# Eleven expert passes whose second layer is seven half-size products

## The chip, the cores and the metric

The program runs on one core of one Trainium2 chip, as one launch. The time is the device time of that core in microseconds (us); the median of three runs of the kernel before is 2035.59 us (2035.21 to 2037.2). Engines: TensorE (PE, with its weight loads PEld), VectorE (DVE), ScalarE (ACT), GpSimd (POOL) and SyncE (SP), which issues the DMA transfers. Inputs and outputs are in HBM, tiles in SBUF, matmul results in PSUM.

## The reference

```python
# q, k, v: (4, 8, 576, 64); heads 0-3 see a band of 32 keys, heads 4-7 every 4th of 128
scores = scale * q @ k.T;  attn = softmax(where(mask, scores, -1e9));  a = attn @ v
x = a.transpose(0, 2, 1, 3).reshape(2304, 512)

P = exp(x @ w_gate - max)                 # (2304, 8), 8 experts
for _ in range(8):                        # Sinkhorn
    P /= P.sum(1, keepdims=True) + 1e-9
    P /= P.sum(0, keepdims=True) + 1e-9
    P *= N / E
out = sum over e of P[:, e:e+1] * (maximum(x @ w1[e], 0) @ w2[e])   # w1 512x1024, w2 1024x512

h = out @ w_in                            # 512x2048
g = where(h >= 1, h, where(h <= -1, 0, (h + 1)**2 / 4))
y = g @ w_out                             # 2048x512, result (2304, 512) float32
```

The last two weight matrices arrive as 64-bit floats and are converted in the kernel.

## The kernel before

The hidden width is cut into units of 512 (`UF`): 16 expert units (two per expert) and 4 units of the final feed-forward layer (FFN). Tokens go in three passes of 768 (`PASS`), halves of 384 (`HALF`) and tiles of 128. Every fp32 operand is split into a high and a low fp32r part; `product` (L267) multiplies them with three matmuls: high x high, high x low, low x high.

Unit 0 is computed for all tokens beside the attention (`first_unit`), in plain form. Every other unit is a run (u, k) of unit u on token pass k: expert units 1 to 15 for k = 0, 1, 2, then the four FFN units for k = 0, 1, 2, 57 runs in all. In a run, `first_layer` makes x times w1 as seven half-size products (a Strassen-Winograd scheme, `ORDER` = 1, 5, 6, 2, 7, 3, 4); the operands of x (`xo`, built once per pass by `build_x`: subtractions on POOL, high parts on ACT, low parts on DVE) and of w1 (`w1o`) are sums and differences of quarters. Results collect in PSUM banks "h" (pa), "t" (pb), "s" and "x" (pc); ACT and DVE join them, and the activation writes the high and low parts of the hidden values into `hs`. `second_layer` then multiplies them by w2 (`w2o`) in plain form: 6 token tiles x 4 chunks x 3 matmuls of 512 columns into six banks; as each tile is complete, DVE scales it by the routing weight and adds it to `acc` (L407), which holds all 18 token tiles in SBUF.

In pass 0 the units are "fresh": w1 and w2 are loaded raw, `prep_w1` (sums on POOL L131, high parts on ACT L104, low parts on DVE L105) and `prep_w2` (L98, L99; quarter by quarter, through a two-quarter stage) make the parts, and these are stored in HBM (`w1_kept`, `w2_kept`) and only reloaded in passes 1 and 2: one 0.5 MB transfer per w1 operand, one of 2 MB for w2. `double_steps` converts the FFN weights in small steps beside runs of pass 1 and 2; `sinkhorn_steps` does the routing iterations beside the runs of units 1 and 2. `turn_steps` (L913) transposes `acc` to be the FFN's input, between the matmuls of a second layer.

The order on each engine is the order of the program text: `tc.manual_schedule()` keeps it, engines take their own instructions in order, and semaphores hold them where data or a buffer are not ready. What runs beside a layer is pulled step by step from generators (`pull`, `drain`) in the loop over `runs`, after each of the 14 turns of a first layer and each of the 24 of a second layer.

## Time and profile before

| | |
|---|---|
| time, median of 3 runs | 2035.59 us |
| the profiled execution | 2036.03 us, span 2034.0 us |
| PE busy | 2003.0 us, 10766 matmuls |
| DVE, ACT, POOL busy | 1182.2, 775.0, 225.9 us |
| granted clock, mean over the span | 0.996 |
| DMA | 425 MB, 209 GB/s |

The span is the time from the first to the last instruction of the profiled execution; the rest of its time lies around it. A busy PE includes the drain of each matmul, which overlaps the next one; the distance from start to start tells its rate. Rows of a DVE or ACT instruction overlap a little in the same way.

### The profile page before, as it was taken

Reading aid. Unit: us, or ns where it says so; the run is one execution under the profiler, and the core shown is the slowest. Engines: PE = TensorE matmul, PEld = TensorE weight load, DVE = VectorE, ACT = ScalarE, POOL = GpSimd, SP = SyncE. Lnnn points to the kernel's source line nnn. Section 1 sums busy time; section 2 is a strip of 40 time slices with the busy share of each in tenths; the row PEclk is TensorE's granted clock in tenths of the full one; section 3 lists DMA queues with packets and bytes.
Section 4 is the critical chain, followed back from the end, with each engine's and each line's share of the span. In section 5 each row is a group of like instructions: output and inputs, shape, how many; then the busy total and the mean of one; then the engine's idle time right before and its main releaser. Section 6 shows DMA issues by size and latency. Waiting matters only on the chain.

```text
span 2034.0 us, 29029 instructions
## 1 busy us (share of the span) xinstructions
PE 2003.0 (98%) x10766; PEld 1803.7 (89%) x10766; DVE 1182.2 (58%) x2334; ACT 775.0 (38%) x1809; POOL 225.9 (11%) x259
## 2 busy tenths in 40 slices
PE   8999989999999999999999999999999999999999
PEld 6888879899998898998998989989989989898898
DVE  6644585766666655664665674633433355655756
ACT  6655434444444423322323323312212334444443
POOL 4212212212212201000002000000000100101000
PEclk9999999999999999999999999999999999999999
DMA  7431256766767665865766867745545446364552
GB/s 170 112 71 50 104 223 243 288 228 258 279 229 261 257 233 212 301 248 227 293 240 233 297 220 270 264 164 203 206 144 220 171 171 227 121 252 156 216 214 87
DMA packets 167501, 425.28 MB, mean 209 GB/s; under 512 B 78529, under 2 KB 78529, under 8 KB 160065
## 3 DMA queue, kind: packets, MB, share of 16 engines
q1 hardware_dynamic: 167360, 423.43, 57.6%
q8 instruction: 85, 1.39, 0.3%
q14 instruction: 56, 0.45, 0.1%
HBM read 309.08 MB, written 114.29 MB: 208 GB/s over the span
## 4 chain that ended last, share of the span: by engine, by line
PE 92%; DVE 4%; ACT 1%; issue 1%; DMA 1%; POOL 0%; DVEq 0%; ACTq 0%; POOLq 0%
PE py L267 46%; PE pa L267 22%; PE pc L267 11%; PE pb L267 6%; PE ph L267 3%; PE s L547 2%; PE px L589 1%; PE pt L515 1%; PE pe L573 1%; DVE r L896 0%; PE pg L680 0%; DVE kept L897 0%; DVE kept L285 0%; DVE hl L901 0%; ACT hh L898 0%
## 5 line engine op out<-in xcount | busy, mean ns | idle before, releaser
L267 PE MATMUL py<-w2o,hh 128*128 128x512 f32 x2736 | 846.2, 390 | 0.0
L267 PEld LDWEIGHTS py<-w2o,hh 128*128 128x128 f32 x2736 | 511.6, 188 | 100.5
L267 PE MATMUL py<-w2o,hl 128*128 128x512 f32 x1368 | 533.0, 390 | 0.0
L267 PE MATMUL pa<-xo,w1o 128*128 128x384 f32 x2736 | 514.9, 335 | 4.6 <-ACT kept L282 3.3
L267 PEld LDWEIGHTS pa<-xo,w1o 128*128 128x128 f32 x2736 | 479.9, 188 | 10.7 <-ACT kept L282 3.7
L282 ACT ACTIVATE kept<-pa 128x384 f32<-128x384 f32 x228 | 112.0, 492 | 556.9 <-PE pa L267 556.2
L407 DVE SCALAR_TENSOR_TENSOR acc<-py,prob,acc 128x512 f32<-128x512 f32 x252 | 178.8, 749 | 236.8 <-PE py L267 232.4
L267 PEld LDWEIGHTS py<-w2o,hl 128*128 128x128 f32 x1368 | 257.1, 188 | 53.6
L267 PE MATMUL pc<-xo,w1o 128*128 128x384 f32 x1368 | 256.7, 335 | 0.7 <-DVE w1o L105 0.7
L267 PEld LDWEIGHTS pc<-xo,w1o 128*128 128x128 f32 x1368 | 239.8, 188 | 1.0 <-DVE w1o L105 1.0
L131 POOL TENSOR_TENSOR raw<-raw 128x256 f32<-128x256 f32 x152 | 130.2, 885 | 873.4 <-DVE raw L213 369.9
L285 DVE TENSOR_TENSOR kept<-pb,kept 128x384 f32<-128x384 f32 x114 | 63.4, 556 | 252.0 <-PE pb L267 251.0
L390 ACT ACTIVATE hh<-kept 128x384 fp32r<-128x384 f32 x270 | 142.1, 526 | 175.3 <-DVE kept L285 174.7
L391 DVE SCALAR_TENSOR_TENSOR hl<-kept,hh 128x384 fp32r<-128x384 f32 x270 | 149.2, 553 | 3.6
L267 PE MATMUL pb<-xo,w1o 128*128 128x384 f32 x684 | 127.7, 334 | 0.0
L267 PEld LDWEIGHTS pb<-xo,w1o 128*128 128x128 f32 x684 | 119.4, 188 | 0.0
L105 DVE TENSOR_TENSOR w1o<-raw,w1o 128x256 fp32r<-128x256 f32 x210 | 97.1, 506 | 27.1 <-ACT w1o L104 27.1
L237 POOL TENSOR_TENSOR xf<-xf 128x768 f32<-128x768 f32 x20 | 37.0, 1870 | 615.1 <-ACT xf L915 612.6
L104 ACT ACTIVATE w1o<-raw 128x256 fp32r<-128x256 f32 x210 | 76.3, 415 | 58.1 <-POOL raw L131 58.1
L99 DVE TENSOR_TENSOR w2o<-raw,w2o 128x512 fp32r<-128x512 f32 x60 | 42.7, 712 | 79.7 <-ACT w2o L98 79.7
L282 ACT ACTIVATE kept<-pc 128x384 f32<-128x384 f32 x114 | 56.2, 493 | 51.1 <-PE pc L267 50.4
L267 PE MATMUL ph<-xo,w1o 128*128 128x384 f32 x288 | 66.9, 358 | 0.0
(139 smaller groups left out, 1670.9 us busy)
## 6 DMA issues: line engine op xcount, KB each, us to landing
w1o<-w_kept SPq DMA_DIRECT2D x294, 512.0 KB, 6.2
w2o<-w_kept SPq DMA_DIRECT2D x42, 2048.0 KB, 7.9
w_kept<-w1o SPq DMA_DIRECT2D x105, 512.0 KB, 4.2
w_kept<-w2o SPq DMA_DIRECT2D x15, 2048.0 KB, 7.3
raw<-in_moe_w_dram SPq DMA_DIRECT2D x15, 1024.0 KB, 6.3
raw<-in_moe_w_dram SPq DMA_DIRECT2D x60, 256.0 KB, 5.5
w_kept<-raw SPq DMA_DIRECT2D x28, 512.0 KB, 2.9
xf<-in_moe_w_in_dram SPq DMA_DIRECT2D x16, 512.0 KB, 5.2
```

What stands on the lines that cost most here:

```text
L99: eng.tensor_tensor(out=lo, in0=raw, in1=hi.bitcast(F32), op=ALU.subtract)
L104: nc.scalar.activation(out=hi, in_=raw, func=AF.Copy)
L105: return lambda: nc.vector.tensor_tensor(out=lo, in0=raw, in1=hi.bitcast(F32), op=ALU.subtract)
L131: nc.gpsimd.tensor_tensor(out=out[:, q], in0=in0[:, q], in1=in1[:, q], op=op)
L237: eng.tensor_tensor(out=o, in0=x, in1=y, op=ALU.subtract)
L267: nc.tensor.matmul(o, lhsT=a(h), rhs=b(l), start=first and n == 0, stop=last and n == 2, skip_group_check=on)
L282: nc.scalar.activation(out=dst, in_=src, func=AF.Copy)
L285: nc.vector.tensor_tensor(out=dst, in0=src, in1=dst, op=ALU.add)
L390: return [lambda: nc.scalar.activation(out=hi, in_=src, func=AF.Relu), lambda: nc.vector.scalar_tensor_tensor(out=lo, in0=src, scalar=0.0, ...
L391: lambda: nc.vector.scalar_tensor_tensor(out=lo, in0=src, scalar=0.0, in1=hi.bitcast(F32), op0=ALU.max, op1=ALU.subtract)]
L407: nc.vector.scalar_tensor_tensor(out=acc[:, t, :], in0=py, scalar=prob[:, t, e:e + 1], in1=acc[:, t, :], op0=ALU.mult, op1=ALU.add)
L547: nc.tensor.matmul(s[:, i, :], lhsT=qd[:, pr, j, :], rhs=kt[:, pr, key0(j):key0(j) + KW], start=not early, stop=not early or i == JG - 1)
```

## The change

Eleven of the expert passes (experts 4 to 7 in pass 1, experts 1 to 7 in pass 2; `WHOLE` names the experts that stay plain in pass 1) are now runs ("e", e, k) of both units of an expert. The two first layers follow each other and leave the hidden values whole in `hid` (ACT only). Then `seven_second` multiplies the 1024-wide hidden matrix by w2 as seven half-size products: 4 chunks x 3 token blocks x 3 matmuls of 256 columns each, into half banks, and DVE adds each block, scaled, to `acc`. The operands of the hidden values are made by `Seven` on DVE (subtractions in place, low parts) and ACT (high parts) at turns written out in `FIRST_WORK` and `SECOND_WORK` (s: subtraction, h: high part, l: low part; operand, piece). Operands rotate through three buffers (`h_buf`, `w2_buf`). The w2 operands come from HBM: quarters from `w2_kept`, now stored in two halves, and four sums from `w2_sums`, which `sum_steps` makes in pass 0 on POOL, ACT and DVE.

To make room, `acc` holds one pass only. First results of unit 0 for passes 1 and 2 go to HBM (`y_kept`) and come back; x of passes 1 and 2 (`x_kept`) and the turned result of each pass (`z_kept`) too. Raw w2 is loaded whole, into `xf`. The operands of a new x are made in place by DVE (`build_in_place`) instead of POOL. The transposes (`turn_steps`) go from the last second layer of a pass into the first layer of the next run, and from bank "h" to "y". The routing iterations get one more turn between the column sum and its matmul, and are pulled in more turns of unit 1. `double_steps` has two stage buffers, fewer pauses, a hold at the end of pass 1, and other turns. Cut to its core:

```diff
-    acc = keep.tile([P, NTILE, DM], F32, name="acc")
+    acc = keep.tile([P, TPP, DM], F32, name="acc")
...
-    w2_kept = [dram.tile([P, 2 * KC * DM], F32, name=f"w2_kept{u}") for u in range(NU)]
+    HD = DM // 2
+    w2_kept = [dram.tile([2, P, 2 * KC * HD], F32, name=f"w2_kept{u}") for u in range(NU)]
+    w2_sums = {e: dram.tile([4, P, 2 * KC * HD], F32, name=f"w2_sums{e}") for e in range(1, E)}
+    x_kept = {k: dram.tile([P, KC * PASS], F32, name=f"x_kept{k}") for k in range(1, NPASS)}
+    y_kept = {k: dram.tile([P, TPP, DM], F32, name=f"y_kept{k}") for k in range(1, NPASS)}
+    z_kept = [dram.tile([P, KC * PASS], F32, name=f"z_kept{k}") for k in range(NPASS)]
...
-    def prep_w2(u, stage):
...
+    def raw_w2(u):
+
+        n = KC * DM
+        at_ = u % 4 * n if u > 1 else KC * PASS
+        return xf.rearrange("p k c x -> p (k c x)")[:, at_:at_ + n]
+
+    def load_raw_w2(u):
+        nc.sync.dma_start(out=raw_w2(u).rearrange("p (c f) -> p c f", c=KC), in_=unit_sources(u)[1])
+
+    def prep_w2(u):
+        for c in TURNS:
+            split(raw_w2(u)[:, c * DM:(c + 1) * DM], (w2o[:, 0, c, :], w2o[:, 1, c, :]), nc.vector)
+            yield
+        for d, (there, here) in enumerate(w2_halves(u)):
+            if d == 0 or u % 2 or u // 2 in WHOLE:
+                nc.sync.dma_start(out=there, in_=here)
 
     TURNS = (0, 2, 1, 3)
 
     def load_w1(u, i):
...
+    SUMS = (7, 6, 5, 3)
+
+    def load_op(e, i, into):
+
+        src = {1: (2 * e, 0), 2: (2 * e + 1, 0), 4: (2 * e + 1, 1)}.get(i)
+        there = w2_sums[e][SUMS.index(i)] if src is None else w2_kept[src[0]][src[1]]
+        nc.sync.dma_start(out=into, in_=there)
+
+    def sum_steps(e, stages):
+
+        n = KC * DM
+        at_ = 2 * e % 4 * n
+        raw = (xf.rearrange("p k c x -> p (k c x)")[:, at_:at_ + 2 * n]
+               .rearrange("p (k c d f) -> p k c d f", k=2, c=KC, d=2))
+        stages = [t[:, :2 * KC * HD].rearrange("p (h c f) -> p h c f", h=2, c=KC) for t in stages]
+        a11, a12, a21, a22 = (raw[:, k, :, d] for d in range(2) for k in range(2))
+        for n_, (out_, in0, in1, op) in enumerate(((a21, a11, a21, ALU.subtract), (a22, a22, a21, ALU.subtract),
+                                                   (a11, a22, a11, ALU.add), (a12, a12, a22, ALU.subtract))):
+            o = stages[n_ % 2]
+            for c in (slice(0, 2), slice(2, 4)):
+                nc.gpsimd.tensor_tensor(out=out_[:, c], in0=in0[:, c], in1=in1[:, c], op=op)
+                yield
+            yield
+            for c in (slice(0, 2), slice(2, 4)):
+                low = high(out_[:, c], (o[:, 0, c], o[:, 1, c]))
+                yield
+                low()
+            nc.sync.dma_start(out=w2_sums[e][n_], in_=words(o).rearrange("p h c f -> p (h c f)"))
...
+    class Seven:
+
+
+
+        def __init__(self, quarters_, into, pieces):
+            b11, b12, b21, b22 = quarters_
+            self.sums = {5: (b11, b12, b11), 6: (b11, b22, b11), 7: (b12, b22, b12), 4: (b21, b21, b11)}
+            self.of = {1: b11, 5: b11, 6: b11, 2: b21, 7: b12, 3: b22, 4: b21}
+            self.into, self.lows = into, {}
+            n = b11.shape[1] // pieces
+            self.cut = [slice(x * n, (x + 1) * n) for x in range(pieces)]
+
+        def sum(self, i, x):
+            dst, in0, in1 = (t[:, self.cut[x]] for t in self.sums[i])
+            nc.vector.tensor_tensor(out=dst, in0=in0, in1=in1, op=ALU.subtract)
+
+        def hi(self, i, x):
+            c, o = self.cut[x], self.into(i)
+            self.lows[i, x] = high(self.of[i][:, c], (o[:, 0, c], o[:, 1, c]))
+
+        def low(self, i, x):
+            self.lows.pop((i, x))()
+
+    def build_in_place():
+        v = xf[:, 0].rearrange("p (k c) (j x) -> p k j c x", k=2, j=2)
+        x = Seven([v[:, kk, j] for kk in range(2) for j in range(2)], lambda i: xo[i], 1)
+        for i in ORDER:
+            for step in (x.sum, x.hi, x.low):
+                if step != x.sum or i in x.sums:
+                    step(i, 0)
+                    yield
...
+    WHOLE = (1, 2, 3)
+
+    FIRST_WORK = {1: "h10 h11", 2: "l10", 3: "l11", 4: "s50", 5: "s51 h50", 6: "h51", 7: "l50", 8: "l51",
+                  12: "s60 s61", 13: "s70 s71"}
+    SECOND_WORK = {(0, 0): "h60 h61", (0, 1): "l60", (0, 2): "l61 h20 h21", (1, 0): "l20", (1, 1): "l21",
+                   (1, 2): "h70 h71", (2, 0): "l70", (2, 1): "l71", (2, 2): "h30 h31", (3, 0): "l30 s40",
+                   (3, 1): "l31 s41", (3, 2): "h40 h41", (4, 0): "l40", (4, 1): "l41"}
+
+    def work(ops, what):
+        for x in what.split():
+            {"h": ops.hi, "l": ops.low, "s": ops.sum}[x[0]](int(x[1]), int(x[2]))
+
+    def seven_second(e, k, buf):
+
+
+        def halves(tags):
+
+            a, b = (bank(t, m, f"q{t}") for t, m in tags)
+            return [a[:, :HD], b[:, :HD], a[:, HD:]]
+
+        chain = {}
+        for n, i in enumerate(ORDER):
+            if i in (1, 5, 2):
+                chain[i] = halves({1: (("y", 2), ("y", 2)), 5: (("t", 2), ("t", 2)), 2: (("s", 1), ("x", 1))}[i])
+            of = {1: 1, 6: 1, 7: 1, 4: 1, 5: 5, 3: 5, 2: 2}[i]
+            d, j = {1: (0, 0), 5: (1, 1), 6: (0, 1), 2: (0, 0), 7: (1, 1), 3: (0, 1), 4: (1, 0)}[i]
+            a, w = buf(n)
+            for t in range(TPH):
+                o = chain[of][t]
+                ts_ = slice(t * P, (t + 1) * P)
+                for c in range(KC):
+                    product(o, lambda h: a[:, h, c, ts_], lambda h: w[:, h, c, :],
+                            of == i and c == 0 and t < 2, c == KC - 1, of != i or t == 2)
+                x = j * TPH + t
+                at_ = acc[:, x, d * HD:(d + 1) * HD]
+                nc.vector.scalar_tensor_tensor(out=at_, in0=o, scalar=prob[:, k * TPP + x, e:e + 1], in1=at_,
+                                               op0=ALU.mult, op1=ALU.add)
+                yield n, t
...
+    def finish_first(py, t):
+        k, x = divmod(t, TPP)
+        here = acc[:, x, :] if k == 0 else at.stage()
+        nc.scalar.activation(out=here, in_=py, func=AF.Copy)
+        if k:
+            nc.sync.dma_start(out=y_kept[k][:, x, :], in_=here)
...
             nc.vector.tensor_reduce(out=cols, in_=prob.rearrange("p t e -> p e t"), axis=AX.X, op=ALU.add)
             yield
             yield
+            yield
...
+        third = late.tile([P, 2 * KC * HALF], F32R, name="third")
+        w2x = late.tile([P, 2 * KC * HD], F32R, name="w2x")
+        h_buf = [x.rearrange("p (h c x) -> p h c x", h=2, c=KC) for x in
+                 (hs[0].rearrange("p c x -> p (c x)"), hs[1].rearrange("p c x -> p (c x)"), third)]
+        w2_all = w2o.rearrange("p h c f -> p (h c f)")
+        w2_buf = [w2_all[:, :2 * KC * HD], w2_all[:, 2 * KC * HD:], w2x]
...
+        hid = wide.rearrange("p (k j c x) -> p k j c x", k=2, j=2, c=KC)
+
+        def act_kept(half_):
+            def act(src, f, j):
+                return [lambda: nc.scalar.activation(out=hid[:, half_, j, f], in_=src, func=AF.Relu)]
+            return act
...
+        def turn_steps(k, more):
+
+
+            z = xf[:, 1]
             for c in range(KC):
                 for j in range(2):
-                    pt = bank("h", 2, f"p2{c}_{j}")[:, :HALF]
+                    pt = bank("y", 2, f"p2{c}_{j}")[:, :HALF]
                     for t in range(TPH):
-                        nc.tensor.transpose(pt[:, t * P:(t + 1) * P],
-                                            acc[:, k * TPP + j * TPH + t, c * P:(c + 1) * P], ident)
-                    nc.scalar.activation(out=xf[:, k, c, j * HALF:(j + 1) * HALF], in_=pt, func=AF.Copy)
+                        nc.tensor.transpose(pt[:, t * P:(t + 1) * P], acc[:, j * TPH + t, c * P:(c + 1) * P], ident)
+                    nc.scalar.activation(out=z[:, c, j * HALF:(j + 1) * HALF], in_=pt, func=AF.Copy)
                     yield
+            nc.sync.dma_start(out=z_kept[k], in_=z.rearrange("p c x -> p (c x)"))
+            if more:
+                nc.sync.dma_start(out=acc, in_=y_kept[k + 1])
...
+        FFN = range(N_MOE, NU)
+        runs = [("u", u, 0) for u in range(1, N_MOE)]
+        for k in range(1, NPASS):
+            runs += [("u", 1, k)]
+            for e in range(1, E):
+                runs += [("u", 2 * e + i, k) for i in range(2)] if k == 1 and e in WHOLE else [("e", e, k)]
+        runs += [("u", u, k) for k in range(NPASS) for u in FFN]
...
+                if fresh and u > 1:
+                    load_raw_w2(u2)
...
+                if ends:
+                    build = build_in_place()
...
+                    if k == 0 and u < 3 and (m % 2 or u == 1 and m > 5):
+                        at.sink = ("y", 2)
+                        pull(sink)
+                    if m < 10:
+                        pull(carry)
+                    if u > 1 and (m < 6 or m > 11):
+                        pull(double)
+                    if m > 3:
+                        pull(turn)
...
+            e = run[1]
+            if k == 1 and begins(n + 2):
+                at.hold = True
+            elif ends and k > 1:
+                drain(double)
+            nxt = load_steps(2 * e + 1)
+            for m, i in enumerate(first_layer(2 * e, act_kept(0), late)):
+                if m % 2:
+                    pull(nxt)
+                if m < 6 or m > 11:
+                    pull(double)
+                if e == 1 and m >= len(ORDER) * UQ - TPP:
+                    t = m - (len(ORDER) * UQ - TPP)
+                    nc.scalar.activation(out=acc[:, t, :], in_=acc[:, t, :], func=AF.Copy,
+                                         scale=prob[:, k * TPP + t, 0:1])
+            drain(nxt)
+            nxt = load_steps(u2)
+            if ends:
+                while k == 1 and not at.held:
+                    pull(double)
+                load_x(n + 1)
+                build = build_in_place()
+
+            def bufs(n_):
+                x = (ring + n_) % 3
+                return h_buf[x], w2_buf[x].rearrange("p (h c f) -> p h c f", h=2, c=KC)
+
+            made = {i: n_ for n_, i in enumerate(ORDER)}
+            ops = Seven([hid[:, kk, j] for kk in range(2) for j in range(2)], lambda i: bufs(made[i])[0], 2)
+            for m, i in enumerate(first_layer(2 * e + 1, act_kept(1), late)):
+                if m % 2:
+                    pull(nxt)
+                work(ops, FIRST_WORK.get(m, ""))
+                if not ends and m < 2:
+                    pull(double)
+            drain(nxt)
+            for n_, t in seven_second(e, k, bufs):
+                work(ops, SECOND_WORK.get((n_, t), ""))
+                if t == TPH - 1:
+                    later = n_ + 3
+                    if later < len(ORDER):
+                        load_op(e, ORDER[later], words(w2_buf[(ring + later) % 3]))
+                    elif after[0] == "e":
+                        load_op(after[1], ORDER[later - 7], words(w2_buf[(ring + later) % 3]))
+                if not ends and (n_, t) >= (4, 0):
+                    pull(double)
+                if ends and (n_, t) in ((1, 2), (2, 2), (3, 2), (4, 1), (4, 2), (5, 0), (5, 1), (5, 2), (6, 0), (6, 1)):
                     pull(build)
...
+            left = build
+            ring = (ring + 7) % 3
```

## Rows read from the trace of the kernel before

**Rows 1.** The page: busy time by engine, and the chain of waits by line.

```profile
PE 2003.0 (98%) x10766; PEld 1803.7 (89%) x10766; DVE 1182.2 (58%) x2334; ACT 775.0 (38%) x1809; POOL 225.9 (11%) x259
...
PE py L267 46%; PE pa L267 22%; PE pc L267 11%; PE pb L267 6%; PE ph L267 3%; PE s L547 2%; PE px L589 1%; PE pt L515 1%; PE pe L573 1%; DVE r L896 0%; PE pg L680 0%; DVE kept L897 0%; DVE kept L285 0%; DVE hl L901 0%; ACT hh L898 0%
```

**Rows 2.** Busy us by stretch (PE, PEld, DVE, ACT, POOL), then PEclk, DMA share, GB/s.

```profile
718.00:1181.00 463.00, 463.00 (x2339) 420.92 (x2338) 285.43 (x534) 134.53 (x277) 25.90 (x28) 1.00 0.68 255
1181.00:1650.00 469.00, 469.00 (x2379) 426.07 (x2378) 211.59 (x380) 125.08 (x249) 13.19 (x12) 1.00 0.56 204
```

**Rows 3.** Chain of waits, a plain unit of pass 1: start us, length us, what.

```profile
1061.22 2.08 PE pc L267 x12
...
1073.71 16.32 PE py L267 x72
```

**Rows 4.** Chain of waits, in the attention.

```profile
176.56 0.64 PE s L547 x6
```

**Rows 5.** Groups of instructions by shape: count | busy us, mean ns | idle before.

```profile
L407 DVE SCALAR_TENSOR_TENSOR acc<-py,prob,acc 128x512 f32<-128x512 f32 x252 | 178.8, 749 | 236.8 <-PE py L267 232.4 <-ACT acc L406 3.8
L391 DVE SCALAR_TENSOR_TENSOR hl<-kept,hh 128x384 fp32r<-128x384 f32 x270 | 149.2, 553 | 3.6
...
L547 PE MATMUL s<-kt,qd 128*128 128x96 f32 x288 | 43.2, 290 | 2.1 <-DVE kt L519 2.1
...
L105 DVE TENSOR_TENSOR xo<-xf,xo 128x768 fp32r<-128x768 f32 x38 | 35.7, 965 | 14.1 <-ACT xo L104 14.1
...
L104 ACT ACTIVATE xo<-xf 128x768 fp32r<-128x768 f32 x38 | 30.8, 837 | 0.0
...
L207 DVE SCALAR_TENSOR_TENSOR xf<-xf 128x512 f32<-128x512 uint32 x32 | 22.0, 688 | 0.7
...
L99 POOL TENSOR_TENSOR w1o<-acc,w1o 128x512 fp32r<-128x512 f32 x3 | 3.8, 1272 | 1.7 <-DVE w1o L96 1.7
```

**Rows 6.** Chain of waits in unit 1, DVE back to back.

```profile
257.75 0.47 DVE kept L285
258.21 0.46 DVE hl L391
```

**Rows 7.** The page, DMA issues: count, KB each, median us to landing.

```profile
w1o<-w_kept SPq DMA_DIRECT2D x294, 512.0 KB, 6.2
w2o<-w_kept SPq DMA_DIRECT2D x42, 2048.0 KB, 7.9
...
raw<-in_moe_w_dram SPq DMA_DIRECT2D x15, 1024.0 KB, 6.3
```

**Rows 8.** Timeline of SP, last FFN unit of pass 0: start us, length us, what.

```profile
1713.22 12.80 SPq L167 DMA_DIRECT2D w1o<-w_kept  x7
```

**Rows 9.** Busy us by stretch: pass 0, unit 1, last FFN unit.

```profile
392.73:409.05 16.32, 16.32 (x74) 13.52 (x73) 12.85 (x22) 5.71 (x16) 5.19 (x6) 1.00 0.93 339
...
237.43:260.48 23.05, 17.90 (x92) 16.83 (x90) 15.86 (x40) 9.88 (x23) 4.45 (x5) 0.93 0.68 257
260.48:285.26 24.78, 20.23 (x83) 15.45 (x83) 23.30 (x74) 6.39 (x18) 4.57 (x6) 0.93 0.55 206
...
1711.08:1725.70 14.62, 14.62 (x86) 14.62 (x85) 7.11 (x15) 6.47 (x13) 0.00 (x0) 1.00 0.89 338
1725.70:1746.15 20.45, 19.50 (x97) 15.61 (x96) 12.69 (x23) 8.83 (x18) 3.95 (x3) 1.00 0.12 41
```

**Rows 10.** Timelines of PE and ACT in unit 1: idle time before and releaser in brackets.

```profile
251.73 2.00 PE L267 MATMUL pa<-xo,w1o 128*128 128x384 f32 x6 [3.33 <-ACT kept L282]
...
264.97 0.39 PE L725 MATMUL psum<-cols,ones 128*128 128x8 f32 x2 [1.61 <-DVE hl L391]
...
250.67 0.63 ACT L98 ACTIVATE w2o<-raw 128x512 fp32r<-128x512 f32 x1 [6.15 <-DMA raw<-in_moe_w_dram]
```

**Rows 11.** PE's waits in 1600 to 2034 us: total, times, longest.

```profile
PE p L913 <- DVE r L897: 1.9, 2, 1.0
```

**Rows 12.** Chain of waits, a turn between matmuls.

```profile
1608.07 0.33 PE p L913 x3
```

More of the change, by code (lines that the diff above doesn't have):

```diff
@@ L167, in load_w1, with w2_halves @@
         nc.sync.dma_start(out=words(w1o[i]).rearrange("p h q c f -> p (h q c f)"), in_=w1_kept[u][i - 1])
+    def w2_halves(u):
+        w = words(w2o).rearrange("p h c (d f) -> p d (h c) f", d=2)
+        return [(w2_kept[u][d].rearrange("p (a f) -> p a f", f=HD), w[:, d]) for d in range(2)]
     def load_w2(u):
[L170 removed]
+        for there, here in w2_halves(u):
+            nc.sync.dma_start(out=here, in_=there)
+    SUMS = (7, 6, 5, 3)
[23 more added lines that the diff above has]
+            yield
     def double_steps(scr, stage1, stage2):
@@ L186, in load @@
             nc.sync.dma_start(out=raws[n % 2], in_=src)
+        loaded = 0
         load(0)
-        for _ in range(8):
+        for _ in range(14):
             yield
         for n, (u, m, c) in enumerate(pieces):
-            if n + 1 < len(pieces):
+            while at.hold:
+                loaded = -1
+                at.held = True
+                yield
+            at.held = False
+            if loaded < n:
+                load(n)
+                for _ in range(8):
+                    yield
+            loaded = n
+            if n + 1 < len(pieces) and not at.hold:
+                loaded = n + 1
                 load(n + 1)
@@ L769, in first_weights @@
             def first_weights():
-                raw = acc[:, 0:4, :], acc[:, 4:8, :]
+                raw = acc[:, 0:4, :], at.big[:, 0:4, :]
                 nc.sync.dma_start(out=raw[0], in_=unit_sources(0)[0])
```

233 lines of the change are left out of this document (128 added, 105 removed).

## The prediction

> **What bounds the kernel now.** I read the page's busy shares first: TensorE (PE) is busy for 2003.0 of 2034.0 us, VectorE (DVE) for 58% and ScalarE (ACT) for 38% [rows 1]. Busy PE rows need not be PE at its limit, so the chain of waits comes next: 46% of the span is the line of second-layer products (py), 22, 11 and 6% are the first layer's pa, pc and pb [rows 1]. The table by stage then shows two stages of 463 and 469 us in which PE has no idle time and its granted clock is 1.00, the level of 2.4 GHz [rows 2]. The chain piece by piece shows one unit of them: seven first-layer products of 2.08 us, then a second layer of 16.32 us, back to back [rows 3]. There, time falls only with PE's own columns and matmuls; work of the other engines is free until PE has to wait for it.
>
> **The price of a matmul.** A first-layer product is 12 matmuls of 384 columns, 2.08 us, 173.3 ns each; a second layer is 72 of 512 columns in 16.32 us, 226.7 ns each [rows 3]. The difference, 53.3 ns for 128 columns, is one column per 2.4 GHz cycle; left over at either width are 13.3 ns per matmul. So I take 256 columns as 106.7 + 13.3 = 120.0 ns. No matmul of this kind with 256 columns is in the trace, so both bounds come from neighbours. Every matmul loads its own weights: six of the attention's, with the same 128x128 weights and only 96 columns, take 0.64 us, 107 ns each [rows 4, 5]; if load and fixed part don't overlap, that makes 120 to 124 ns. From below, 106.7 ns are the columns alone.
>
> TensorE: Matmul & The Clock Gate in the Trainium skill (section Back-to-back issue gap) gives columns/2.4 + 2.5 ns for warm matmuls. By that rule, an estimate of 109.2 ns for 256 columns, the sum would end near 1975 us. The two widths of rows 3 carry 13.3 ns and not 2.5, so the row decides.
>
> **Eleven expert passes.** The new loop runs experts 4 to 7 of token pass 1 and 1 to 7 of pass 2 as one step of two units; experts 1 to 3 of pass 1 stay plain (WHOLE). The first layers stay, 2 x 14.6 us. The two second layers, 144 matmuls of 512 columns, 32.64 us, become 7 products x 3 token blocks x 4 chunks x 3 = 252 matmuls of 256 columns, 252 x 0.120 = 30.24 us: 2.40 us less for each pass, **26.4 us for eleven**. Columns fall by an eighth, but the 13.3 ns are paid 108 times more.
>
> What a pass adds beside PE has to fit into its 59.4 us. On DVE, 384-column operations follow each other at 0.465 us though their rows say 0.55 [rows 5, 6], so I charge each row less 0.09 us. Gone: 16 low parts (0.47) and 12 finishing operations (749 ns, so 0.66). Added: 21 finishing operations of 256 columns (between half of 0.66 and 0.47; I take 0.41), 14 low parts and 8 subtractions of 768 columns (965 ns, so 0.87). DVE goes from some 21 to 33 us, plus up to 19 steps of the FFN weights' conversion at 0.6 at most (688 ns) [rows 5]. ACT gets 14 high parts of 768 columns (837 ns). Neither is full over a pass.
>
> The tight places are local. In the second unit's first layer DVE has 6 adds, 6 subtractions, 4 low parts and 2 conversion steps: 2.8 + 5.2 + 3.5 + 1.2 = 12.7 of 14.6 us; four of the subtractions are issued after the last add that PE waits for, so a delay goes into the second layer. There a product lasts 36 x 0.12 = 4.32 us and its operand is split one product ahead or more: the third product's last low part is due at 8.64 us, issued at 4.3, done by some 6. Blocks 0 and 2 of a product now share a PSUM bank, so block 2 can have to wait until DVE has read block 0: slack 1.44 - 0.41 = 1.0 us, which two low parts with two subtractions (turns 9 and 10, 4.3 us of DVE in 2.9) nearly use up. Cost taken: 0. Bound: 0.6 us (one conversion step too many) in the nine passes with conversion, 5 us. Below nothing is excluded, as no DVE work leaves PE's path.
>
> PSUM — Partial Sum Buffer in the Trainium skill (section PSUM bank collisions raise a hardware error) forbids two engines in one bank at once, in whatever columns. It speaks for that wait; no run here shows its price.
>
> A new wait: operand n+3's weight part (1 MB) goes into the buffer of operand n, so SP issues it when PE ends product n, and it is due 8.64 us later. Behind it on SP stand the next part and the conversion's transfers; behind a late one stands PE. Transfers land 6.3 us after issue for 1 MB, 6.2 for 0.5 and 7.9 for 2 MB [rows 7]; I take 6.5, hidden. The pass moves 14 x 0.5 + 7 x 1 MB in 59.4 us, 247 GB/s; the stage before carries 255 [rows 2]. First layers now follow each other directly, so a w1 part reloaded after its product is due some 12 us later, against 6.2: hidden.
>
> **Pass 0.** POOL makes the sums of w2 (8 operations of 512 columns per expert, nearest row 1272 ns [rows 5]), with 8 high and 8 low parts. A second layer there has DVE at 12.85 of 16.32 us [rows 9]; five low parts of 0.6 make it 15.9, and a rest can slip into the next first layer. Cost 0; bound 1 us for each of seven experts. The stores (4 MB more per expert, about 1 MB no longer kept) go out while nobody waits for them.
>
> **The first unit after the attention.** Unit 1 takes 23.05 + 24.78 = 47.8 us [rows 9] instead of the 30.9 of rows 3. DVE is busy for 39 us of it, mostly with the routing iterations. PE waits 3.33 us behind an ACT that stood 6.15 us for the raw w2, and then for the iterations, 1.61 us at one of them [rows 10]; the granted clock is 0.93 in the mean [rows 9]. Raw w2 is now loaded whole, long before. An iteration gets three turns between its column sum and its matmul instead of two, and about one of eight moves into unit 2. I take 40 us, DVE's 39 less one iteration (2.3) plus some waits: **-8 us**; bounds 0 (the waits only move) and -12. The stores of x ahead of the raw load, 3 MB, are done long before that load's first use: 0.
>
> **Turns and boundaries.** The three rounds of transposes of acc stay, 8 x 0.33 us each [rows 12], but go into the next first layer, with bank "y". Two waits for the FFN activation there, 1.9 us [rows 11], go: **-2 us** (0 to -2). The subtractions for a new x go from POOL to DVE, 4 x 0.87 = 3.5 us at five boundaries; in the last FFN unit of a pass DVE is busy for 7.1 of 14.6 and 12.7 of 20.5 us [rows 9]: **+2** (0 to +5). Staging the first results of passes 1 and 2 through two buffers, and bank "h", which ACT must now empty between two first layers: **+3** (0 to +6).
>
> **Sum**, against the profiled execution (2036.03 us: span 2034.0 and 2.0 around it; the median shown is 0.4 lower): 2036.0 - 26.4 - 8 - 2 + 2 + 3 = **2004.6, forecast 2005 us**.
>
> **The rivals.**
> *B, the narrow matmul costs 124 ns* (load and fixed part in a row): 11 x 252 x 0.004 = 11 us more, **2016**. For it: 107 ns of load stand beside 106.7 of columns. Against: a load that starts with the matmul before is done before 120 ns. The passes break even at 32.64/252 = 129.5 ns. 15%.
> *C, unit 1 keeps its length*: **2013**. For: DVE is busy for 23.3 of 24.8 us in its second half [rows 9]. 12%.
> *D, the ring of three is late: slower than before.* Four operands of each pass, 44 in all, must land inside the second layer; the other three have two first layers. Each us beyond 8.64 costs 44 us; the gain of 31 us is gone at a landing of 8.64 + 31/44 = 9.35 us, and 10 us make **2065**. For: SP issues in order, seven loads spread over 12.80 us as PE frees their tiles [rows 8], and 2 MB need 7.9 us. Against: 1 MB needs 6.3, and one part is asked for per 4.32 us. 8%.
> *E, the fixed part is not paid at this width* (106.7 ns): 252 x 0.1067 = 26.9 us a pass, 37 us less, **1968**. Against: it is equal at two widths. 3%.
> *F, DVE is late* at the bounds above (5 + 7 us): **2017**. 9%.
> *G, the change does not do what it says*: 256 columns last as long as 512, 11 x 252 x 0.107 = 297 us more. Nothing speaks for it but that the width is new. 1%.
>
> **How the numbers follow.** Forecast 52%, between 1999 and 2011. With B, C and F the time lies from 1995 to 2024, some 85%; what is left out is E below, D, G and mixtures above. Within 0.2%, 4 us, about what a measurement of this kernel can tell from no change, only B, C and F together or a small D end: 3%. Slower: most of D, and G: 8%. Faster: 89%.
>
> **What would show it.** In the profile after: 2772 matmuls of 256 columns, 252 in a chain of some 30.2 us (B: 31.2; E: 26.9). PE without idle time in passes 1 and 2; a wait of PE for a low part or for acc there is F, for a transfer into the w2 buffers D. Unit 1 near 40 us, with no wait of ACT for raw w2. Transposes without a wait for r. The prediction is wrong if the narrow matmul exceeds 129 ns or operands land after 9 us.

## The result, and the profile after

The changed kernel takes 2009.7 us (median of four runs, 2007.84 to 2019.49) against 2035.78 us in the same session: ratio 0.9879, 95% interval 0.9866 to 0.9892, so 24.6 us or 1.2% less (below, too, a ratio is to the kernel before in the same session). The forecast was 2005. The profiled execution took 2011.22 us with a span of 2009.4; before, the span was 2034.0 us, again 24.6 us more. Some runs, of the kernel before too, lie some 8 us above the rest, at a lower mean clock, and widen the intervals.

The page after, busy time by engine and the chain by line (as rows 1):

```profile
PE 1976.8 (98%) x11954; PEld 1839.1 (92%) x11954; DVE 1423.2 (71%) x2575; ACT 916.4 (46%) x2019; POOL 282.3 (14%) x295
...
PE py L350 28%; PE pa L350 22%; PE pc L350 10%; PE qy L350 9%; PE pb L350 5%; PE qt L350 5%; PE ph L350 3%; PE s L679 2%; PE qs L350 1%; PE px L721 1%; DVE xf L323 1%; PE pe L705 1%; PE pt L647 1%; PE qx L350 1%; DMA w1o<-w_kept 1%
```

PE is as full as before, with 1188 matmuls more. DVE went from 58 to 71%. New are qy, qt, qs and qx, the blocks of the seven products; py fell from 46 to 28%. Two lines in the tail are new: DVE xf L323, the subtractions, and DMA w1o, each with 1% of the chain.

The chain piece by piece in an expert pass of token pass 1 (start us, length us, what), to be read beside rows 3:

```profile
1025.19 4.31 PE qy L350 x36
1029.51 4.32 PE qt L350 x36
...
1038.13 1.42 PE qs L350 x12
...
1055.36 2.11 PE pa L350 x12
```

A product of 36 matmuls takes 4.31 us, 119.7 ns each. The whole second layer, from 1025.03 us to 1055.20, takes 30.17 us for 252 matmuls, where two plain ones take 2 x 16.32 [rows 3].

Busy time by stretch (PE, PEld, DVE, ACT, POOL, then PEclk, DMA share, GB/s): an undisturbed second layer, one with a wait, then the first pair of first layers, the first layer into the FFN and one at an FFN boundary:

```profile
1025.03:1055.20 30.17, 30.17 (x254) 30.17 (x254) 24.30 (x41) 9.43 (x14) 0.00 (x0) 1.00 0.69 239
1143.67:1174.45 30.78, 30.42 (x254) 30.22 (x254) 26.67 (x41) 11.56 (x15) 0.00 (x0) 1.00 0.58 203
...
934.83:965.74 30.91, 29.72 (x169) 29.11 (x168) 22.03 (x37) 16.77 (x33) 0.00 (x0) 1.00 0.97 372
1625.26:1645.06 19.80, 17.94 (x111) 16.89 (x110) 14.47 (x26) 12.76 (x26) 0.00 (x0) 1.00 0.63 219
1754.52:1770.75 16.23, 14.87 (x86) 14.54 (x84) 12.65 (x22) 7.38 (x14) 0.00 (x0) 1.00 0.82 284
```

Where the length exceeds PE's busy time, PE waited, and it lost somewhat more than that: the second row has 0.36 us without PE and is 0.61 longer than the first. Its waits in the eleven passes, 934 to 1626 us, and then from 1626 us to the end (who, for what: us in total, times, longest; kept L365 is ACT's copy of a result out of PSUM, its evacuation):

```profile
PE pa L350 <- DMA w1o<-w_kept: 1.1, 1, 1.1
PE qy L350 <- DVE acc L465: 0.7, 2, 0.4
PE qt L350 <- DVE acc L465: 0.3, 1, 0.3
PE pa L350 <- ACT xf L1064: 0.2, 1, 0.2
```

```profile
PE pa L350 <- ACT kept L365: 2.7, 2, 1.4
PE p L1075 <- ACT xf L1076: 1.9, 2, 1.2
```

In 692 us of passes PE's own waits are 2.3 us, and none is for a transfer into a w2 buffer. Four of the eleven second layers are longer than 30.17 (30.78, 30.70, 30.51, 30.78); three hold the waits for acc (L465), DVE's additions of finished blocks, and into the fourth, at 1296.67 us, the chain comes over four subtractions (L323) and then an addition too. In the first of them the chain goes over three subtractions, the last of which stands here (start us, length us, what):

```profile
1162.97 0.87 DVE xf L323
1163.84 0.40 DVE acc L465
1164.24 0.04 issue
1164.29 1.70 PE qy L350 x12
```

PE's last block of a product starts when DVE has added the first one, from the same bank.

Unit 1 after the attention, its two layers (as rows 9):

```profile
239.88:262.80 22.92, 17.91 (x92) 16.70 (x90) 18.65 (x47) 10.91 (x25) 4.00 (x5) 0.93 0.80 279
262.80:282.37 19.57, 17.84 (x81) 14.27 (x81) 18.64 (x53) 5.45 (x15) 4.87 (x6) 1.00 0.65 248
```

It takes 42.5 us instead of 47.8. PE's longest waits in it are now for the column sums of the routing iterations:

```profile
PE psum L858 <- DVE cols L853: 4.9, 3, 3.2
```

The page's transfers by size and landing (as rows 7):

```profile
w1o<-w_kept SPq DMA_DIRECT2D x294, 512.0 KB, 6.1
w2o<-w_kept SPq DMA_DIRECT2D x58, 1024.0 KB, 5.9
...
w2o<-w_sums SPq DMA_DIRECT2D x32, 1024.0 KB, 5.0
```

**Where the 24.6 us come from**, stretch by stretch, as lengths after minus before: start of unit 1, 239.88 against 237.43, +2.45; unit 1, -5.35; the eleven second layers, 333.96 against 22 x 16.32, -25.1; their first layers, +1.95; turns and boundaries, +2.05; the last second layer, -0.45. Sum -24.5.

### The profile page after: what moved, and what is told of

Same layout as the page of the kernel before. It is cut to its first block, busy times and chain, and to the rows that moved or that the text cites. A ratio compares the mean times of both kernels' runs of the same rounds, so it can differ in the third digit from the quotient of the medians.

```text
span 2009.4 us, 32018 instructions
## 1 busy us (share of the span) xinstructions
PE 1976.8 (98%) x11954; PEld 1839.1 (92%) x11954; DVE 1423.2 (71%) x2575; ACT 916.4 (46%) x2019; POOL 282.3 (14%) x295
## 4 chain that ended last, share of the span: by engine, by line
PE 89%; DVE 6%; ACT 2%; DMA 2%; issue 1%; POOL 0%; SPq 0%; ACTq 0%; POOLq 0%; DVEq 0%
PE py L350 28%; PE pa L350 22%; PE pc L350 10%; PE qy L350 9%; PE pb L350 5%; PE qt L350 5%; PE ph L350 3%; PE s L679 2%; PE qs L350 1%; PE px L721 1%; DVE xf L323 1%; PE pe L705 1%; PE pt L647 1%; PE qx L350 1%; DMA w1o<-w_kept 1%
## 5 line engine op out<-in xcount | busy, mean ns | idle before, releaser
L350 PE MATMUL py<-w2o,hh 128*128 128x512 f32 x1680 | 517.6, 389 | 0.0
L350 PEld LDWEIGHTS py<-w2o,hh 128*128 128x128 f32 x1680 | 314.6, 188 | 62.5
L350 PE MATMUL py<-w2o,hl 128*128 128x512 f32 x840 | 326.8, 389 | 0.0
L365 ACT ACTIVATE kept<-pa 128x384 f32<-128x384 f32 x228 | 111.7, 492 | 314.0 <-PE pa L350 312.3
L350 PEld LDWEIGHTS py<-w2o,hl 128*128 128x128 f32 x840 | 157.7, 188 | 32.8
L513 ACT ACTIVATE hh<-kept 128x384 fp32r<-128x384 f32 x138 | 72.5, 526 | 100.3 <-DVE kept L368 100.3
L323 DVE TENSOR_TENSOR xf<-xf 128x768 f32<-128x768 f32 x108 | 99.1, 951 | 0.2
L1064 ACT ACTIVATE xf<-kept 128x384 f32<-128x384 f32 x132 | 68.3, 524 | 63.3 <-DVE kept L368 63.1
L539 DVE SCALAR_TENSOR_TENSOR acc<-py,prob,acc 128x512 f32<-128x512 f32 x120 | 84.3, 740 | 9.8 <-PE py L350 9.8
L110 DVE TENSOR_TENSOR third<-xf,third 128x768 fp32r<-128x768 f32 (+1 forms) x82 | 76.7, 943 | 18.4 <-ACT third L109 18.4
L465 DVE SCALAR_TENSOR_TENSOR acc<-qy,prob,acc 128x256 f32<-128x256 f32 x132 | 63.5, 481 | 36.7 <-PE qy L350 33.5
```

Of the source, the lines that this page charges most:

```text
L110: return lambda: nc.vector.tensor_tensor(out=lo, in0=raw, in1=hi.bitcast(F32), op=ALU.subtract)
L323: nc.vector.tensor_tensor(out=dst, in0=in0, in1=in1, op=ALU.subtract)
L350: nc.tensor.matmul(o, lhsT=a(h), rhs=b(l), start=first and n == 0, stop=last and n == 2, skip_group_check=on)
L365: nc.scalar.activation(out=dst, in_=src, func=AF.Copy)
L465: nc.vector.scalar_tensor_tensor(out=at_, in0=o, scalar=prob[:, k * TPP + x, e:e + 1], in1=at_, op0=ALU.mult, op1=ALU.add)
L513: return [lambda: nc.scalar.activation(out=hi, in_=src, func=AF.Relu), lambda: nc.vector.scalar_tensor_tensor(out=lo, in0=src, scalar=0.0, ...
```

## Experiments

Times of single runs scatter by some 2 us and more, mostly in and ahead of unit 1 (below), so the lengths of stretches in the traces carry more than the totals.

**1. Three passes instead of eleven.** Experts 6 and 7 of token pass 1 and expert 7 of pass 2 stay expert passes; the others run as plain units.

```diff
-    WHOLE = (1, 2, 3)
+    WHOLE = (1, 2, 3, 4, 5, 6)
...
-            runs += [("u", 2 * e + i, k) for i in range(2)] if k == 1 and e in WHOLE else [("e", e, k)]
+            runs += [("u", 2 * e + i, k) for i in range(2)] if e in WHOLE[:4 + k] else [("e", e, k)]
```

> Only three expert passes are kept (experts 6 and 7 in pass 1, expert 7 in pass 2); the other eight go back to plain units, everything else stays as changed. Theory (each pass is worth its second layers, 32.64 us down to about 30.2 to 30.4): eight passes fewer give 18 to 20 us back, 2028 to 2030 us against 2009.7 of the change; the remaining 6 to 8 us below the kernel before are those of unit 1 and of three passes. Rival (the gain comes from elsewhere, the freed memory, the whole raw w2 and the new turns, and the passes are worth little because stalls eat them): less than 8 us more, under 2018.

Measured: 2027.13 us (six runs), ratio 0.9952, 0.9928 to 0.9976. Eight passes fewer cost 17.4 us against the changed kernel by the medians and 14.9 by the ratios, 1.9 to 2.2 us each: a little under the 18 to 20 expected, and far from the rival's 8. Most of the gain is in the passes. The 10 us that are left are about what three passes and unit 1 give, less what the turns and boundaries cost; this rest was not taken apart.

**2. Two parts ahead instead of three.** The weight parts are asked for one product later in the program, the three buffers stay.

```diff
-                    for x in range(3):
+                    for x in range(2):
...
-                    later = n_ + 3
+                    later = n_ + 2
```

> The w2 part of product n+2 instead of n+3 is loaded when product n ends, so a part is due 4.3 us after its issue instead of 8.6. Theory (transfers of 1 MB land 5 to 6 us after issue, and the three-deep ring has 2.5 to 3.5 us to spare): PE waits 0.7 to 1.7 us before each of the last five products of a pass, 55 products in all: 40 to 90 us more, 2050 to 2100 us, with PE's waits put down to the DMA into the w2 buffers. Rival (bandwidth alone counts: 1 MB takes 2.5 us at 400 GB/s, the ring's depth is spare): within 5 us of the change.

Measured: 2011.6 us, one run. The theory fell, and the trace tells why: the edit did not shorten the time that most parts have. SP waits for the buffer, not for the place in the program. The part of the fourth product was issued at 1419.06 us, when the first product (from 1414.56) had ended, as in the changed kernel. The chain of the longest second layer, 31.86 us, shows two exceptions:

```profile
1415.12 8.30 DMA w2o<-w_sums
1423.42 0.14 issue
1423.56 4.55 PE qy L350 x36
...
1436.40 5.51 DMA w2x<-w_kept
1441.91 0.14 issue
1442.04 4.54 PE qy L350 x36
```

The first is the third product's part: its place in the program now lies behind the w1 loads on SP, it landed 8.30 us after its issue, and PE waited 0.2 us. The second left SP only behind a store of the conversion (1435.97 us), one product before its use, and PE waited 1.0 us. The experiment says nothing of the third buffer.

**3. Two buffers.** The same with the third buffer taken away, so that a part can be asked for one product before its use and not two.

```diff
-                return h_buf[x], w2_buf[x].rearrange("p (h c f) -> p h c f", h=2, c=KC)
+                return h_buf[x], w2_buf[(ring + n_) % 2].rearrange("p (h c f) -> p h c f", h=2, c=KC)
...
-                    later = n_ + 3
+                    later = n_ + 2
...
-                        load_op(e, ORDER[later], words(w2_buf[(ring + later) % 3]))
+                        load_op(e, ORDER[later], words(w2_buf[(ring + later) % 2]))
...
```

> The weight parts of the seven products go through two buffers instead of three, so the part of product n+2 can be asked for only when product n has ended, and is due one product (4.32 us) later instead of two (8.64). Theory: the ring is kept on time only by its third buffer. In the changed kernel these parts land 4.8 to 5.9 us after issue, and a two-deep ring makes PE wait in three places of each second layer (operands 3, 5 and 7), each for landing minus 4.32: 0.6 to 2.2 us, 33 places, 20 to 70 us more: 2030 to 2080 us, seven-product layers of 32 to 36 us instead of 30.2, with PE waiting for a transfer into w2o or w2x. Rival: with one transfer fewer in flight each lands within 4.3 us; then the time stays within 5 us of 2010.

Measured: 2047.99 us, one run, against 2036.56 before the change in the same session: slower. The second layers take 32.5 to 35.3 us, 37.5 us above eleven times 30.17, and PE's waits there are (total, times, longest):

```profile
PE qy L350 <- DMA w2o<-w_sums: 17.4, 21, 2.0
PE qy L350 <- DMA w2o<-w_kept: 9.9, 11, 1.8
PE qy L350 <- ACT third L109: 0.5, 1, 0.5
```

32 waits of 0.85 us in the mean, at three places of each pass, as the theory had it; landing was 4.8 and 4.9 us in the median against 4.32 due. Rival D's mechanism is real; the third buffer's 8.64 us kept it away here.

**4. A bank for every block.** In products 1, 5 and 2 no two of the three blocks share a PSUM bank.

```diff
-            a, b = (bank(t, m, f"q{t}") for t, m in tags)
-            return [a[:, :HD], b[:, :HD], a[:, HD:]]
+            return [bank(t, m, f"q{t}")[:, :HD] for t, m in tags]
...
+                if i == 5:
+                    both = bank("h", 2, "qh")
+                chain[i] = (halves((("h", 2), ("y", 2), ("y", 2))) if i == 1 else
+                            [both[:, :HD]] + halves((("t", 2), ("t", 2))) if i == 5 else
+                            halves((("s", 1), ("x", 1))) + [both[:, HD:]])
...
```

> Each block of a product gets a PSUM bank that no neighbouring block uses (the two idle banks h are brought in), so block 2 does not wait for DVE to read block 0. Theory (the four passes whose seven products take 30.5 to 30.8 us instead of 30.17 lose the difference to the shared bank when DVE is late): all eleven stand at 30.2, 2.1 us less in all, 2006 to 2009 us, and no wait of PE for acc is left in a pass. Rival (DVE is late for the operands' low parts anyway, the bank only shows it first): the same passes keep 0.3 to 0.6 us, now waiting for a low part.

Measured: 2009.37 us, one run. Ten second layers take 30.16 or 30.17 us and one 30.23, in all 2.1 us less than the 333.96 of the changed kernel. PE's waits in the passes are left with two, none for acc or a subtraction:

```profile
PE pa L350 <- DMA w1o<-w_kept: 0.3, 1, 0.3
PE pa L350 <- ACT xf L1067: 0.2, 1, 0.2
```

So the shared banks are what made DVE's delay into PE's: DVE is as busy (26.6 us of the layer that had 26.67), but nobody waits for it. (The rest of the total went in unit 1, 44.8 us here.)

**5. The routing's turns as before.** Two turns between column sum and matmul, and the old places of the iterations.

```diff
-            yield
             yield
             yield
             pc = bank(*at.sink
...
-                    if k == 0 and u < 3 and (m % 2 or u == 1 and m > 5):
+                    if k == 0 and u < 3 and m % 2:
```

> The routing iterations go back to two turns between column sum and matmul, and to the turns of unit 1 in which they were pulled before; raw w2 stays loaded whole. Theory (unit 1 fell from 47.8 to 42.5 us mainly because ACT no longer stands 6.15 us for raw w2): 42 to 44.5 us for unit 1, the total within 2 us of the change. Rival (the new turns of the iterations brought it): unit 1 goes back to 46 to 48 us, the total to 2013 to 2015.

Measured: 2012.08 us, one run. Unit 1 takes 45.6 us, at nearly the clock of the changed kernel's 42.5 (0.92 and 1.00):

```profile
238.43:259.17 20.74, 17.87 (x92) 16.82 (x91) 16.91 (x39) 9.91 (x23) 4.01 (x5) 0.92 0.80 284
259.17:283.99 24.82, 18.98 (x83) 14.24 (x83) 23.33 (x74) 6.41 (x18) 4.55 (x6) 1.00 0.66 239
```

That is between theory and rival. By these two runs, 3.1 of the 5.35 us go with the turns; but unit 1 scatters by 2.4 us with the same code (last section), so the size is uncertain. The rest, 2.3, stands beside the raw w2 that ACT no longer waits for, which was not tried alone, and beside the clock: the second layer ran at 0.93 before [rows 9] and at 1.00 here, by an estimate from these rows worth up to 1.7 us.

**6. Three repairs.** (a) Weight parts asked for later at the first pass, (b) the transposes into the FFN in fewer gaps, (c) staged results through a space of `xf` taken to be idle.

```diff
-                    for x in range(3):
-                        load_op(after[1], ORDER[x], words(w2_buf[(ring + x) % 3]))
+                    entered = True
...
+                if entered and m in (0, 4, 8):
+                    load_op(e, ORDER[m // 4], words(w2_buf[(ring + m // 4) % 3]))
+                    entered = m < 8
...
-                    if m > 3:
-                        pull(turn)
+                    if m > 3 or kind == "ffn" and m:
+                        pull(turn, 2 if kind == "ffn" else 1)
...
+            return xf[:, 2].rearrange("p c x -> p (c x)")[:, at.staged % 6 * DM:(at.staged % 6 + 1) * DM]
...
```

> Three small edits of the changed kernel, each in its own stretch. (a) At the change from plain units to the first expert pass, the three weight parts of 1 MB are asked for at turns 0, 4 and 8 of the pass's second first layer instead of all ahead of the w1 loads. (b) At the turn into the FFN two groups of transposes go into each gap, from the second product on. (c) The staged results of passes 1 and 2 go through six slots of an idle input half instead of two staging buffers. Theory: (a) the first pair of first layers falls from 30.9 to 29.2 us, -1.2 to -1.7 (w1o landed 10.4 us after issue behind 3 MB); (b) the first layer after the last expert pass falls from 19.8 to about 17.4, -2.4; (c) the first first layer starts 2.4 us earlier (ACT waited 2.42 us for a store of a staged result). In all -5 to -6.5 us: 2003 to 2005. Rival: the waits are only the last of several, and the same layers keep their lengths within 0.5 us, because another transfer or DVE is late next: 2008 to 2011.

Measured: 2014.26 us (four runs), ratio 0.9899, 0.9874 to 0.9923: no gain in the total. In the trace (a) and (b) did what was expected, 30.91 to 29.15 us and 19.80 to 17.89. (c) did not: the space is not idle, since unit 0 still reads x of pass 2 there. So this kernel computes pass 2 from overwritten input, and its first layer of unit 1 starts at 243.98 us, 4.1 later than in the changed kernel. The price of the staging stays open.

**7. Fourteen passes.** Experts 1 to 3 of pass 1 as passes too, with the conversion pulled in more of their turns, and in more turns of unit 1 in pass 2.

```diff
-    WHOLE = (1, 2, 3)
+    WHOLE = ()
...
-                    if m > 12 or u > 1 and m % 5:
+                    if m > 12 or (u > 1 or k == 2) and m % 5:
                         pull(double)
...
-                if m < 6 or m > 11:
-                    pull(double)
+                pull(double)
...
-                if not ends and (n_, t) >= (4, 0):
+                if not ends and ((n_, t) >= (4, 0) or (n_, t) in ((0, 0), (1, 2), (2, 2))):
                     pull(double)
...
```

> Experts 1 to 3 of token pass 1 are made expert passes too (14 instead of 11); the conversion of the FFN weights, which went beside the plain units, is pulled in more of the passes' turns. Theory: a pass is 2.1 us shorter than two plain units whatever its expert, so three more give -6 to -7.5 us: 2002 to 2004, if DVE has room. DVE is busy for some 36 of 59 us in a pass here. Rival: the conversion's steps in the turns make DVE late; PE waits for acc, a low part or an add in each of the passes with conversion, 0.5 us or more for each of ten, and the gain is gone: 2008 to 2014 us.

Measured: 2013.19 us (four runs), ratio 0.9886, 0.9871 to 0.99: the rival's time, but only in part its cause. The three added second layers take 30.2 to 30.4 us, but PE's waits from 714 to 1630 us are now (total, times, longest)

```profile
PE pa L350 <- ACT xf L1064: 3.1, 4, 0.9
PE pa L350 <- ACT kept L365: 2.8, 1, 2.8
PE pa L350 <- DMA w1o<-w_kept: 1.8, 1, 1.8
PE qy L350 <- DVE acc L465: 0.7, 2, 0.4
```

and DVE, ahead of the pair of first layers that takes 37.45 us instead of 29.2, waited for

```profile
DVE xf L246 <- DMA xf<-in_moe_w_out_dram: 12.7, 1, 12.7
```

A step of the conversion, pulled in the plain unit 1 of pass 2 before its source had landed (13.2 us after its issue), held DVE and every addition behind it; ACT's next conversion step waited for DVE, and the evacuations stood behind that. PE's two waits in this pair are 4.6 us of the 8.3 lost. A product after each of them takes 3.7 us instead of 2.08, at a mean granted clock of 0.55 and 0.54. So the largest loss lies in one place, at the change to the passes, and begins with a step in a plain unit's turns; the four waits in the passes (L1064), 3.1 us, are nearer to the rival's cause. Whether fourteen passes gain with that step in another place stays open.

**8 and 9. The repairs together.** Experiments 4, 6a and 6b, and a fourth repair for the two waits for ACT's evacuation at the FFN boundaries.

> The changed kernel with four repairs, each in its own stretch: own bank for every block (e3_own_banks: all seven-product layers 30.17 us, -2.1); weight parts asked for during the pass's second first layer (first pair of first layers 30.9 to 29.2 us, -1.7); two groups of transposes per gap at the turn into the FFN (19.8 to 17.9 us, -1.9); and the rest of an input's making at a boundary starts with the fourth product of the next first layer instead of the first. Theory for the last: at 1758.5 and 1884.2 PE waits 1.36 us for ACT's evacuation of pa, which stands in ACT's queue behind a high part that waits 3.8 us for a subtraction on DVE; with the rest issued later these two first layers fall from 16.2 to 14.6-15.0 us, -2.4 to -3.3. In all -8 to -9 us: about 2001, 2000 to 2003. Rival for the last: DVE itself is late there (the acc additions), so the later subtraction delays another operand and the two layers stay near 16; then 2004 to 2006.

```diff
-                    if m < 10:
+                    if m > 2:
                         pull(carry)
```

Measured: 2013.97 us (six runs), ratio 0.9891, 0.9873 to 0.9908, above both forecasts. The fourth repair was wrong twice. At the turn into the FFN it delayed operands that are due at once (25.32 us instead of 17.9; PE's waits from 1620 to 1650 us):

```profile
PE pa L350 <- ACT xo L109: 4.0, 1, 4.0
PE pa L350 <- DVE xo L110: 1.3, 1, 1.3
PE pc L350 <- DVE xo L110: 0.3, 1, 0.3
```

At the FFN boundaries nothing changed (16.24 and 16.22), for in ACT's timeline the blocking instruction stands in front of the evacuations there, issued at the end of the second layer (start us, length us; idle before, releaser):

```profile
1762.22 0.84 ACT L109 ACTIVATE xo<-xf 128x768 fp32r<-128x768 f32 x1 [3.83 <-DVE xf L323]
1762.97 0.85 ACT L365 ACTIVATE kept<-pa 128x384 f32<-128x384 f32 x2
```

So that second layer now leaves the last five steps over:

```diff
-                    if ends and m > 4 and (m % 2 if kind == "ffn" else m % 3 == 0):
+                    if ends and m > 4 and (m % 2 and m < 17 if kind == "ffn" else m % 3 == 0):
...
-                    if m < 10:
+                    if m > 2 or n and input_of(runs[n - 1])[1] != "ffn":
                         pull(carry)
```

> As e8_four_repairs, but its fourth repair is placed otherwise. There the delay of the rest cost 6.6 us at the turn into the FFN (PE waited 4.0 us for ACT's high part and 1.5 us for a low part), and the two FFN boundaries stayed at 16.2: the high part in front of ACT's evacuation is issued at the end of the second layer, not in the next first layer. Now the last five steps of an input's making are left over at the FFN boundaries alone, and issued from the fourth product of the next first layer on; the other boundaries are as in the changed kernel. Theory: the first layers at the two FFN boundaries fall from 16.2 to at most 15.0 us (-2.4 in all), the one into the FFN is near 17.9 (-1.9), the first pair of first layers 29.2 (-1.7), the seven-product layers 30.17 (-2.1). In all -8 us against 2010: 2000 to 2004. Rival: DVE's own acc additions or the subtraction bind at the boundaries: the two layers stay above 15.7, the time is 2004 to 2007.

Measured: 2005.38 us (five runs, 2002.08 to 2009.92), ratio 0.9846, 0.9829 to 0.9862: below both kernels, though above the 2000 to 2004 expected. The first pair, a second layer, the turn into the FFN and the two boundaries:

```profile
937.38:966.50 29.12, 29.12 (x169) 29.12 (x168) 22.04 (x37) 16.74 (x33) 0.00 (x0) 1.00 0.93 346
1144.43:1174.59 30.16, 30.16 (x253) 30.16 (x253) 26.59 (x41) 11.56 (x15) 0.00 (x0) 1.00 0.60 205
1623.96:1641.83 17.87, 17.87 (x110) 16.88 (x109) 10.74 (x19) 11.38 (x23) 0.00 (x0) 1.00 0.79 273
1751.36:1766.59 15.23, 14.86 (x86) 14.41 (x84) 12.66 (x22) 7.67 (x14) 0.00 (x0) 1.00 0.91 318
1876.13:1890.86 14.73, 14.73 (x86) 14.57 (x84) 12.21 (x21) 7.67 (x14) 0.00 (x0) 1.00 0.91 313
```

The four repairs show 1.8, 2.1, 1.9 and 2.5 us, 8.3 in all, where they were made. The span is 5.6 us shorter, since unit 1 took 44.6 us here and began 0.4 later.

## Why the prediction was right, step by step

The median, 2009.7, lies within the 1999 to 2011 of the forecast; the profiled execution, 2011.22, is just outside it.

**The matmul.** 120.0 ns was forecast from two wider widths, 119.7 measured: 13 ns beyond the columns at this width too. B (124) and E (106.7) are out. B's price was not worked out, though: 107 + 13.3 is 120.3, so the measured time does not tell the forecast from the lower end of "120 to 124". TensorE: Matmul & The Clock Gate in the Trainium skill (section Back-to-back issue gap) gives columns/2.4 + 2.5 ns for a warm matmul, as the gap of an isolated one: an estimate of 109.2 ns for 256 columns. The trace does not agree: 119.7 ns in a full stream.

**Eleven passes.** Forecast -26.4; -25.1 in the second layers, where undisturbed ones gain 2.47 each and the four late ones give back 2.1. The first layers give back 1.95, which had no term: at the first pass the w1 part that PE waited 1.1 us for stood behind 3 MB of w2 parts and landed 12.3 us after its issue at 938.3 us, against 6.2 [rows 7]. That a w1 part is "due some 12 us later, against 6.2: hidden" held nearly everywhere else; the step left out what SP issues at the change from plain units. Experiment 6a gives 1.8 us of it back.

**DVE's tight places.** Cost 0 with a bound of 5 us; it was 2.1, in four passes and not nine. The place was right: block 2 waiting for DVE's reading of block 0, in one bank. The reason given, "one conversion step too many", was right for at most half of it: two of the four, 30.78 us each, are the last pass of a token pass, in whose second layer the program pulls no conversion but the making of the next input, and there the third subtraction in the chain is the next input's. DVE is busy for 39 to 41 us of an undisturbed pass, within the 33 plus at most 11 charged, and the finishing operation takes 0.40 us in the chain (0.41). PSUM — Partial Sum Buffer in the Trainium skill (section PSUM bank collisions raise a hardware error) forbids two engines in one bank at once. The trace agrees so far that PE waits: by 0.3 to 0.4 us in the rows, with layers 0.3 to 0.6 us longer, and experiment 4 shows that own banks remove it.

**The ring.** D got 8% and did not come; the parts land 4.8 to 5.9 us after issue (medians by kind) of the 8.64 that they have. With 4.32 us left it does come, and at 2048 us ends slower than before.

**Unit 1.** Forecast -8, bounds 0 and -12; measured -5.35. PE no longer waits behind an ACT that stands for raw w2, but 4.9 us, 3.2 at the longest, for the column sums of the iterations on DVE. "DVE's 39 less one iteration (2.3) plus some waits" put the waits too low: 37.3 us of DVE are in 42.5, which leaves 5.2 for waits where the 40 had 3.3. And the profiled run is on the short side: six of the eight kernels named below have 44.5 to 44.8 us there, at a lower clock, so the step was worth some 3 to 5 us against the one trace of before.

**Turns and boundaries.** Forecast -2 + 2; measured +2.05. The two waits for the FFN's activation went [rows 11], and the same 1.9 us came back as waits of the transposes for ACT's copies (L1076). At the two FFN boundaries PE now waits 2.7 us for ACT: an evacuation stood in its queue behind a high part, and that behind a subtraction on DVE. Before, these two waits were short, and for DVE:

```profile
PE pa L267 <- DVE kept L285: 0.7, 2, 0.3
```

The term had the subtractions' work but not that queue. Experiment 9, which moves the high part out of the way, shows it: 2.5 us less in these two layers.

**Staging.** Forecast +3; unit 1 began 2.45 us later, and ACT did wait 2.42 us for a store of a staged result. But in eight kernels with the same code up to there (the changed one, experiments 1 to 4, 7, 8 and 9, numbered as above) it began between 236.3 and 241.0 us, so one trace can't tell it from scatter, and experiment 6c left it open. The cost of staging is argued, not shown. Pass 0 cost nothing, as forecast: PE lost no time there to DVE or POOL.

So the terms were off by +1.3, +1.95, +2.65 and +2.05 us, 8 us towards less gain; the staging, 0.55 under its term, and the last second layer, 0.45 shorter, take 1 us back. That makes up 2005 against 2011 for the profiled execution, to 0.4 us. Only the first of the four has a loss in the steady part, 2.1 us, and over half of that is at the end of a token pass; the others are in unit 1 and at changes between stages. The price of the matmul, which carries the forecast, was right by its reason. That four misses towards less gain ended at the edge of the range and not beyond it is partly luck.

## What to carry to other kernels

Where PE is full, price an exchange of few wide matmuls for many narrow ones by the fixed part per matmul, taken from two widths in the trace; it held to 0.3% at a third. It was not tried below 256 columns, and the attention's matmuls of 96 columns, 107 ns each [rows 4], do not follow it: 40 + 13.3 would be 53. Then count the changes between stages with the same care as the steady loop: what each in-order queue has in front of the first item that somebody waits for. And the deadline of most parts here was set by the release of a buffer, not by the place of the instruction in the program: an experiment on it must take a buffer away.

## What was not expected of the hardware

The clock makes unit 1 uncertain. In the changed kernel and in the last experiment PE has nearly the same two waits early in it (0.6 and 1.2 us). The granted clock in the 2 us that follow the second one, first in the changed kernel and then in the last experiment:

```profile
246.00:248.00 2.00, 2.00 (x14) 2.00 (x13) 1.43 (x3) 2.00 (x6) 0.00 (x0) 1.00 0.79 307
```

```profile
246.00:248.00 2.00, 1.99 (x6) 1.99 (x7) 1.44 (x4) 2.00 (x5) 0.00 (x0) 0.50 0.59 236
```

In the one the clock stays at 2.4 GHz, in the other it is at 1.2, and twelve matmuls of 384 columns take 3.0 instead of 2.1 us. Around the later wait of 3.2 us it fell to 0.50 in both. Over the eight traces with the same code unit 1 takes 42.4 to 44.8 us, so a difference of 2 us between single runs of these kernels is not by itself an effect.
